# Batch 0 of a fused cross-attention and SiLU MLP kernel: loads issued ahead of a hold, one state loaded in fp32, the first activation split, and a rewritten order of two matmul streams

## The chip, the cores and the metric

The kernel runs on one core of one Trainium2 chip. The core has five engines that run side by side: TensorE (PE, with its weight loads shown as PEld), VectorE (DVE), ScalarE (ACT), GpSimd (POOL) and SyncE (SP, which here only issues transfers). They wait for one another through semaphores. The metric is the device time of one execution in microseconds (us); lower is better. A profiled execution gives a trace whose span is a little shorter than that time.

## What is computed

```python
# x: (8, 8, 512, 64)  batch, head, token, depth      state: (8, 8, 32, 64)
a  = softmax(x @ state^T / 8);   xread = a  @ state          # 512 rows of each head
a2 = softmax(state @ x^T / 8);   sread = a2 @ x              # 32 rows of each head
X  = concat([xread, sread], rows), heads side by side        # (8 * 544, 512)
h  = X @ w_in                    # w_in  (512, 2048)
out = (h * sigmoid(h)) @ w_out   # w_out (2048, 512), out (4352, 512), fp32
```

## The kernel before

**Folding.** For the 512 token rows of a batch, h = a @ (state @ w_in). The kernel forms W1[b] = state @ w_in (256 rows, heads times states, by 2048) and multiplies the normalised attention weights by it, so that only 256 rows are summed where w_in has 512. `w1_mms` and `w1_out` make W1 in column pieces of 512 (one piece needs the same columns of w_in; ScalarE and VectorE copy it out of PSUM).

**G1 and G2.** The 2048 columns are 16 slices of 128 (`ft`). `emit_G1(k)` makes slice k: two matmuls of 512 columns into a PSUM tile (two buffers take turns), and a silu on ScalarE into `g`. `upto(k)` emits all slices below k that are still to do. `G2(0, tt, ft)` multiplies 128 rows (`tt` 0 to 3) of slice ft by w_out and adds to one of four PSUM tiles. Batch 0 takes this plain form, because its weights are still arriving. From batch 1 on, G2 is a two-level Strassen-like product: `t_weights` and `inner_weights` make differences of w_out on VectorE once, and the `Unit` class runs seven products, their steps threaded between the next G1 by a list `todo` of (product, step, earliest slice).

**Order.** The schedule is by hand: each engine runs its instructions in the order of the program text. The start is lines 176 to 281. SP loads x[0] in two halves of four heads (L186). GpSimd makes the identity, sets columns of ones beside x[0] (`ones_beside_x`, L193), issues w_in columns 0 to 255 and 256 to 511, w_out slices 0 and 1, and state 1, which is cast to bf16 while it is loaded (L197). Then a one-element copy, `after_casts` (L279), reads the last piece of x[0] that VectorE casts; it holds GpSimd's queue until that is there. Behind it come w_out 2 and 3 and w_in 512 to 1023 (L280, 281), then two parts of the softmax normalisation of batch 0 (`an`, L400), then w_out 4 to 7, w_in 1024 on, x[1], and the rest of the weights (L874 to 883). There are eight semaphores for GpSimd's loads, so that each load from the ninth on waits for the landing of the one eight before it.

`g1_first` (L536) makes the first two slices, with a silu of 512 columns each. The loop at L908 then goes through slices 0 to 11 of batch 0. `LEAD0` says how far G1 runs ahead, `W0` and `W1_AT` at which slice a W1 piece of batches 0 and 1 is made (before slices 3, 6 and 11), `T3` when the fourth row tile takes its G2. The transposes, scores and exponentials of batch 1 stand at slices 8 to 10. After the loop come the remaining G2 and four G1 slices with transposes of batch 1's attention weights between them; then four `inner_weights`, of which two are made here (L956) and two in batch 1 (L1059).

Of the kernel before, what the change touches and what calls it, by code (L numbers as in the profile page):

```python
# [22 lines left out]
D = 64  # L23
# [19 lines left out]
def kernel(  # L43
# [37 lines left out]
    ident = pers.tile([128, 128], BF16)  # L81
    st_b = pers.tile([128, 8, 2 * D], BF16)
    st0_f = pers.tile([128, 2, D], FP32)
    st1_n = pers.tile([128, 2, D], BF16)
    st0_n = pers.tile([128, 2, D], BF16)

# [32 lines left out]
    def ones_beside_x(i, eng):  # L119
        eng.memset(  # L120
            x_rows[i][:, 0 : 16 * XW].rearrange("p (i w) -> p i w", w=XW)[:, :, 0:PAD], 1.0
        )
        eng.memset(x_rows[i][:, ds(16 * XW, PAD)], 1.0)
# [32 lines left out]
    def load_w_in(f, n=512):  # L156
        nc.gpsimd.dma_start(w_in_sb[:, :, ds(f, n)], win_re[:, :, ds(f, n)])

    def load_w_out(g0, n):
        nc.gpsimd.dma_start(w_out_sb[:, ds(g0, n), :], wout_re[:, ds(g0, n), :])  # L160
# [24 lines left out]
    for hg in range(2):  # L185
        nc.sync.dma_start(  # L186
            x_f[0][:, ds(4 * hg, 4), :, :],
            x[0, ds(4 * hg, 4)].rearrange("h (p c) d -> p h c d", p=128, c=4),
        )
    nc.vector.memset(stT[:, 0], 0.0)  # L190
    nc.vector.memset(stT[:, 1:8], 0.0)
    make_identity(nc, ident)
    ones_beside_x(0, nc.gpsimd)  # L193
    load_w_in(0, 256)
    load_w_in(256, 256)
    load_w_out(0, 2)
    nc.gpsimd.dma_start(  # L197
        st1_n.rearrange("p v d -> p (v d)"),
        state[1].rearrange("h (m v) d -> (h m) (v d)", v=2),
    )  # L200

    both = (nc.vector, nc.scalar)

    def load_states():
        nc.gpsimd.dma_start(
            st_b[:], state.rearrange("b h (n2 m v) d -> (b h n2) m (v d)", n2=2, m=8)
        )
# [69 lines left out]
        cast_x(0, eng, c, n, 4, 4)  # L277
    after_casts = pers.tile([128, 1], BF16)
    copy(nc.gpsimd, after_casts[:], x_nat[0][:, 2, 3, 127:128])  # L279
    load_w_out(2, 2)  # L280
    load_w_in(512)

    st_x = pers.tile([128, 8, B, 4, 2, 2], BF16)

# [199 lines left out]
    def w1_mms(b, cols, new=bank):  # L484
        pss = {}
        if b not in W1:
            W1[b] = wpool.tile([128, 2, DF], BF16, tag="W1", name="W1")
        for f, n in cols:
            for hg in range(2):
                pss[f, hg] = new([128, 512], FP32, "ps_w1")  # L490
            for s in range(4):
                for hg in range(2):
                    h = HEAD_OF_SLOT[hg][s]
                    r = 64 * (h % 2)
                    nc.tensor.matmul(  # L495
                        pss[f, hg][ds(32 * s, 32), 0:n],
                        stT[ds(r, 64), b, h // 2, s % 2, :],
                        w_in_sb[ds(r, 64), h // 2, ds(f, n)],
                        start=True,
                        stop=True,  # L500
                        tile_position=(r, 32 * s),
                        skip_group_check=True,
                    )
# [15 lines left out]
    gt = {}  # L519
# [16 lines left out]
    def g1_first():  # L536
        for k in range(2):
            g_tile(k)
        pss = [
            psA.tile([128, 512], FP32, tag="a1", name="h1"),  # L540
            psH.tile([128, 512], FP32, tag="h1", name="h1"),
        ]
        for hg, c, n in ((0, 0, 4), (1, 0, 2), (1, 2, 2)):
            for k in range(2):
                nc.tensor.matmul(
                    pss[k][:, ds(128 * c, 128 * n)],
                    W1[0][:, hg, ds(128 * k, 128)],
                    aT[0][:, hg, ds(c, n), :],
                    start=(hg == 0),
                    stop=(hg == 1),  # L550
                    skip_group_check=True,
                )
        for k in range(2):
            nc.scalar.activation(gt[k], pss[k][:], func=SILU, bias=0.0)

    def g1_half(k, hg):
        b, ft = divmod(k, NFT)
# [342 lines left out]


    turn[0] = 0
    W0 = {3: (512, 512), 6: (1024, 512), 11: (1536, 512)}
    W1_AT = {3: 0, 6: 512, 11: 1024}
    LEAD0 = [3, 3, 2, 1, 4, 3, 2, 3, 4, 3, 2, 1]
    T3 = {1: (0, 1), 2: (2,), 3: (3,), 4: (4,), 5: (5,), 6: (6,), 7: (7,), 10: (8,)}
    ready = 4
    for ft in range(12):  # L908
        upto(min(ft + LEAD0[ft], ready))
        if ft == 1:  # L910
            place_one_state(1, transpose_one_state(st1_n), nc.vector)
        if ft in W0:
            pss = w1_mms(0, [W0[ft]], new_h)
            pss1 = w1_mms(1, [(W1_AT[ft], 512)])
            w1_out(0, [W0[ft]], both, pss)
            if ft == 6:
                cast_x(1, nc.vector, 2, 2, 0, 4)
            w1_out(1, [(W1_AT[ft], 512)], both, pss1)
            ready = sum(W0[ft]) // 128
        if ft == 5:  # L920
            t_weights((1,), 0, 8)
        if ft == 6:
            for hg in range(2):
                cast_x(1, nc.gpsimd, 0, 2, 4 * hg, 4)
            load_states()
            load_x(2)
            cast_x(1, nc.vector, 2, 2, 4, 4)
            load_x(3)
        if ft == 8:
            for hg in range(2):  # L930
                pe_transpose_x(1, hg, 1, engs=(nc.vector,))
            nc.scalar.activation(warm[:], busy[:, 0:1], func=EXP, bias=0.0)
        if ft in (9, 10):
            scores(1, ft - 9, new=new_h)
            exps(1, ft - 9)
        if ft == 9:
            t_weights((2, 3, 4), 0, 4)
        if ft == 10:
            nc.scalar.activation(warm[:], busy[:, 0:1], func=SILU, bias=0.0)
            norm(1, 0)  # L940
        if ft == 11:
            norm(1, 1, ((nc.vector, 0, 4),))
# [55 lines left out]
    for b in range(1, B):  # L998
# [41 lines left out]
        for j in range(lead, NFT):  # L1040
            upto(NFT * b + j + 1)
            if j == 8:
                u.hi = gh[b, 1]
            if j == max(lead, 5):
                u.sums3(0, 4)
                if b == 1:
                    transpose_x(3)
                    for v in range(2):
                        evict_state(v, (nc.vector, nc.gpsimd)[v], 2, 2)
                if inner:  # L1050
                    u.inner_sums((3,))
# [172 lines left out]
```

## Time and profile before

| what | us |
|---|---|
| median of three runs | 201.53 (201.41 to 201.54) |
| the profiled execution | 201.34 |
| its span in the trace | 199.5 |
| TensorE busy in the span | 191.3 |
| VectorE, ScalarE, GpSimd busy | 149.1, 139.0, 73.3 |
| moved by DMA over the span | 28.72 MB |

The granted TensorE clock is full in all slices of the span. Busy time counts a matmul from its start to its modelled end, and successive matmuls overlap, so a gap between two rows of the timeline can be longer than the idle time printed in brackets. A few matmul records are missing from a trace.

### The profile page before, as it was taken

The numbers are of one execution on the slowest core, as the hardware profiler recorded it, in microseconds if no ns is written. First come the engines' busy times: TensorE is split into PE (matmuls) and PEld (weight loads), VectorE is DVE, ScalarE is ACT, GpSimd is POOL, SyncE is SP. The second block draws the span as 40 slices with busy tenths as digits, with TensorE's granted clock in tenths as the row PEclk, the third lists the DMA queues.
The fourth block names the chain that finished last, engine by engine and source line by source line (L and its number), as shares of the span: only waits on it lengthen the run. The fifth ranks groups of instructions, "written<-read, shape, count | busy, mean of one in ns | idle before, by whom it ended". The sixth has DMA issues, their size and how long they took to land.

```text
span 199.5 us, 4817 instructions
## 1 busy us (share of the span) xinstructions
PE 191.3 (96%) x1962; PEld 130.3 (65%) x1980; DVE 149.1 (75%) x284; ACT 139.0 (70%) x254; POOL 73.3 (37%) x98
## 2 busy tenths in 40 slices
PE   7799999999999999999999999999999999999992
PEld 2343354467766677667766777668766876788881
DVE  3854579897899799869995879769676997673072
ACT  2865597689779797889778967889588167825530
POOL 7596452497593008500760047102400236002200
PEclk9999999999999999999999999999999999999999
DMA  5999999999459463495229930952090005000143
GB/s 187 195 168 213 294 206 321 223 298 214 150 91 275 109 214 58 165 228 189 53 108 218 259 59 0 291 97 52 4 264 3 5 12 210 3 0 0 41 174 105
DMA packets 40839, 28.72 MB, mean 144 GB/s; under 512 B 27377, under 2 KB 37489, under 8 KB 40817
## 3 DMA queue, kind: packets, MB, share of 16 engines
q1 hardware_dynamic: 34592, 20.52, 39.3%
q0 software_dynamic: 5936, 7.64, 18.7%
q8 instruction: 15, 0.25, 0.5%
q10 hardware_dynamic: 288, 0.26, 0.4%
q14 instruction: 8, 0.06, 0.1%
HBM read 17.43 MB, written 8.91 MB: 132 GB/s over the span
## 4 chain that ended last, share of the span: by engine, by line
PE 76%; DMA 13%; DVE 6%; issue 1%; ACT 1%; POOL 0%; SPq 0%; DVEq 0%; ACTq 0%
PE o L686 35%; PE h L560 21%; DMA w_in_sb<-in_moe_w_in_dram 10%; PE h L578 4%; PE ps_w L495 3%; PE o L749 3%; DMA x_f<-in_x_dram 3%; DVE W L166 2%; PE o_ch L749 2%; PE o_s L806 2%; DVE g L611 2%; PE o L806 1%; PE ps_sr L434 1%; PE o_a L597 1%; PE o L597 1%
## 5 line engine op out<-in xcount | busy, mean ns | idle before, releaser
L588 ACT ACTIVATE g<-h 128x512 bf16<-128x512 f32 (+1 forms) x142 | 80.0, 574 | 30.2 <-PE h L560 13.0
L560 PE MATMUL h<-aT,W 128*128 128x512 bf16 x237 | 69.7, 379 | 0.2
L686 PEld LDWEIGHTS <-g 128*128 128x128 bf16 x464 | 44.8, 98 | 20.9 <-DVE kept L614 0.7
L686 PE MATMUL o<-w_out_sb,g 128*128 128x256 bf16 x336 | 49.0, 273 | 0.4
L614 POOL TENSOR_TENSOR o_sb<-o_sb,kept 128x512 f32<-128x512 f32 x7 | 10.3, 1473 | 76.3 <-ACT o_sb L164 76.3
L560 PEld LDWEIGHTS <-W 128*128 128x128 bf16 x252 | 23.1, 98 | 7.5 <-issue 0.9
L686 PE MATMUL o<-wt,s 128*128 128x256 bf16 x224 | 27.3, 273 | 0.0
L686 PEld LDWEIGHTS <-s 128*128 128x128 bf16 x224 | 21.5, 98 | 4.5 <-issue 2.1
L166 DVE CAST W<-ps_w 128x512 bf16<-128x512 f32 (+1 forms) x34 | 21.1, 665 | 3.3 <-PE ps_w L495 3.2
L164 ACT ACTIVATE W<-ps_w 128x512 bf16<-128x512 f32 (+1 forms) x32 | 16.8, 582 | 7.9 <-PE ps_w L495 7.9
L166 POOL CAST x_nat<-x_f 128x512 bf16<-128x512 f32 x24 | 16.0, 707 | 6.2 <-DMA x_f<-in_x_dram 6.2
L614 DVE TENSOR_TENSOR o_sb<-o_sb,o 128x512 f32<-128x512 f32 x14 | 9.6, 683 | 11.2 <-PE o L686 7.5
L686 PE MATMUL o<-wt,g 128*128 128x256 bf16 x128 | 16.8, 273 | 0.0
L611 DVE TENSOR_TENSOR g<-g 128x1024 bf16<-128x1024 bf16 x15 | 11.2, 744 | 6.5 <-ACT g L588 6.3
L164 ACT ACTIVATE o_sb<-o 128x512 f32<-128x512 f32 x15 | 8.9, 595 | 8.7 <-PE o L686 4.5
L614 POOL TENSOR_TENSOR o_sb<-kept,o_sb 128x512 f32<-128x512 f32 x7 | 9.2, 1311 | 15.4 <-ACT o_sb L164 15.4
L611 DVE TENSOR_TENSOR g<-g,s 128x1024 bf16<-128x1024 bf16 x14 | 14.4, 1071 | 0.0
L611 DVE TENSOR_TENSOR s<-g 128x512 bf16<-128x512 bf16 (+3 forms) x23 | 11.0, 508 | 0.0
L749 PEld LDWEIGHTS <-inner 128*128 128x128 bf16 x96 | 7.3, 98 | 5.4
L495 PE MATMUL ps_w<-w_in_sb,stT 64*32 64x512 bf16 (+1 forms) x264 | 10.2, 375 | 0.6 <-DMA w_in_sb<-in_moe_w_in_dram 0.5
L597 PEld LDWEIGHTS <-g 128*128 128x128 bf16 x64 | 5.7, 98 | 7.0 <-issue 1.2
L614 DVE TENSOR_TENSOR s<-s,g 128x1024 bf16<-128x1024 bf16 x15 | 9.7, 686 | 0.0
(123 smaller groups left out, 256.3 us busy)
## 6 DMA issues: line engine op xcount, KB each, us to landing
out_dram<-o_sb SPq DMA_DIRECT2D x14, 512.0 KB, 2.8
x_f<-in_x_dram SPq DMA_DIRECT2D x6, 512.0 KB, 5.2
w_out_sb<-in_moe_w_out_dram POOLq DMA_DIRECT2D x8, 256.0 KB, 9.5
x_f<-in_x_dram POOLq DMA_DIRECT2D x2, 1024.0 KB, 11.9
x_f<-in_x_dram SPq DMA_DIRECT2D x2, 1024.0 KB, 5.8
w_in_sb<-in_moe_w_in_dram POOLq DMA_DIRECT2D x3, 512.0 KB, 9.2
x_f<-in_x_dram POOLq DMA_DIRECT2D x2, 512.0 KB, 10.3
out_dram<-o_sb SPq DMA_DIRECT2D x4, 256.0 KB, 6.0
```

The lines of the kernel that those rows point to most:

```text
L164: nc.scalar.activation(dst, src, func=COPY, bias=0.0)
L166: eng.tensor_copy(dst, src)
L495: nc.tensor.matmul(pss[f, hg][ds(32 * s, 32), 0:n], stT[ds(r, 64), b, h // 2, s % 2, :], w_in_sb[ds(r, 64), h // 2, ds(f, n)], start=True, ...
L560: nc.tensor.matmul(h_ps[k][:], W1[b][:, hg, ds(128 * ft, 128)], aT[b][:, hg, :, :], start=(hg == 0), stop=(hg == 1), skip_group_check=True,)
L578: nc.tensor.matmul(ps[:, 0:256], w_in_sb[:, kt, ds(128 * ft, 128)], xmT[:, :, kt].rearrange("p t n b -> p t (n b)"), start=(kt == 0), stop ...
L588: nc.scalar.activation(gt[k], ps[:, 0:n], func=SILU, bias=0.0)
L597: nc.tensor.matmul(outs[tt][:], gt[b * NFT + ft][:, ds(128 * tt, 128)], w_out_sb[:, ft, :], start=(ft == 0), stop=(ft == NFT - 1), skip_gr ...
L611: eng.tensor_tensor(dst, a, c, op=SUB)
L614: eng.tensor_tensor(dst, a, c, op=ADD)
L686: nc.tensor.matmul(to[:, t, :], left[:, ds(128 * t, 128)], right[:, k, :], start=first and t == 0, stop=(k == 7), skip_group_check=True,)
L749: nc.tensor.matmul(to, left[:, k], right[:, k], start=where not in self.begun, stop=(k == 3), skip_group_check=True,)
L806: nc.tensor.matmul(to[:, 0:n], left[:, k], right[:, k, ds(c, n)], start=(first and k == 0), stop=(k == 7), skip_group_check=True,)
```

## The change

1. Of GpSimd's start, the columns of ones go to VectorE. In front of the hold stand now five weight loads (w_in 0 and 256, w_out 0 to 3, w_in 512), behind it w_out 4 to 7. State 1 is loaded in fp32 by SP after x[0]; GpSimd casts it after the normalisation.
2. The first silu of `g1_first` is two instructions of 256 columns.
3. The tables of the batch 0 loop are replaced. W1's columns 1024 are made after the first G2 of slice 6 and columns 1536 after the fourth row tile's slice 7, behind the loop; that tile's slices 6 to 11 all move behind the loop. At slice 8 each half of batch 1's transposes follows a pair of G1.
4. Batch 0's two `inner_weights` join those of batch 1. In batch 2 step 4 of product 1 moves ahead, from slice 13 to slice 9.

```diff
-    make_identity(nc, ident)
-    ones_beside_x(0, nc.gpsimd)
+    nc.sync.dma_start(
+        st1_f.rearrange("p v d -> p (v d)"),
+        state[1].rearrange("h (m v) d -> (h m) (v d)", v=2),
+    )
...
+    ones_beside_x(0, nc.vector)
+    make_identity(nc, ident)
     load_w_in(0, 256)
     load_w_in(256, 256)
     load_w_out(0, 2)
-    nc.gpsimd.dma_start(
-        st1_n.rearrange("p v d -> p (v d)"),
-        state[1].rearrange("h (m v) d -> (h m) (v d)", v=2),
-    )
+    load_w_out(2, 2)
+    load_w_in(512)
...
     copy(nc.gpsimd, after_casts[:], x_nat[0][:, 2, 3, 127:128])
-    load_w_out(2, 2)
-    load_w_in(512)
+    load_w_out(4, 2)
+    load_w_out(6, 2)
...
-        for k in range(2):
-            nc.scalar.activation(gt[k], pss[k][:], func=SILU, bias=0.0)
+        for k, c, n in ((0, 0, 256), (0, 256, 256), (1, 0, 512)):
+            nc.scalar.activation(
+                gt[k][:, ds(c, n)], pss[k][:, ds(c, n)], func=SILU, bias=0.0
+            )
...
-    load_w_out(4, 2)
-    load_w_out(6, 2)
+    copy(nc.gpsimd, st1_n[:], st1_f[:])
     load_w_in(1024)
...
-    W0 = {3: (512, 512), 6: (1024, 512), 11: (1536, 512)}
-    W1_AT = {3: 0, 6: 512, 11: 1024}
-    LEAD0 = [3, 3, 2, 1, 4, 3, 2, 3, 4, 3, 2, 1]
-    T3 = {1: (0, 1), 2: (2,), 3: (3,), 4: (4,), 5: (5,), 6: (6,), 7: (7,), 10: (8,)}
-    ready = 4
+    def w_pieces(f, f1):
+        pss = w1_mms(0, [(f, 512)], new_h)
+        pss1 = w1_mms(1, [(f1, 512)])
+        w1_out(0, [(f, 512)], both, pss)
+        if f == 1024:
+            cast_x(1, nc.vector, 2, 2, 0, 4)
+        w1_out(1, [(f1, 512)], both, pss1)
+
+    UPTO = {0: 3, 1: 4, 4: 8}
     for ft in range(12):
-        upto(min(ft + LEAD0[ft], ready))
+        upto(UPTO.get(ft, 0))
...
+        if ft == 3:
+            w_pieces(512, 0)
...
         if ft == 8:
-            for hg in range(2):
-                pe_transpose_x(1, hg, 1, engs=(nc.vector,))
+            upto(10)
+            pe_transpose_x(1, 0, 1, engs=(nc.vector,))
+            upto(12)
+            pe_transpose_x(1, 1, 1, engs=(nc.vector,))
...
         for tt in range(3):
             G2(0, tt, ft)
-        for i in T3.get(ft, ()):
-            G2(0, 3, i)
-    transpose_states()
-    for ft in (9, 10):
+            if ft == 6 and tt == 0:
+                w_pieces(1024, 512)
...
+        if 0 < ft < 6:
+            for i in ((0, 1) if ft == 1 else (ft,)):
+                G2(0, 3, i)
+    for ft in range(6, 12):
         G2(0, 3, ft)
+        if ft == 7:
+            w_pieces(1536, 1024)
+            norm(1, 1, ((nc.vector, 0, 4),))
+            transpose_states()
     upto(14)
     pe_transpose_a(1, 0, nc.vector)
-    G2(0, 3, 11)
     upto(16)
     pe_transpose_a(1, 1, nc.vector)
     t_weights((3, 2, 4), 4, 4)
-    for i in (0, 1):
-        inner_weights(i, nc.vector)
...
-            todo = [(1, k - 8, k + 4) for k in range(4)] + [(7, 1, 8)]
+            todo = [(1, k - 8, k + 4) for k in range(4)] + [(7, 1, 8), (1, -4, 9)]
...
-            todo += [(1, k - 8, (k + 23) // 2) for k in range(4, 8)]
+            todo += [(1, k - 8, (k + 23) // 2) for k in range(5, 8)]
...
-                    for i in (2, 3):
+                    for i in range(4):
                         inner_weights(i, nc.vector)
```

More of the change, by code (lines that the diff above doesn't have):

```diff
@@ L83 @@
     st0_f = pers.tile([128, 2, D], FP32)
+    st1_f = pers.tile([128, 2, D], FP32)
     st1_n = pers.tile([128, 2, D], BF16)
@@ L902 @@
     turn[0] = 0
-    W0 = {3: (512, 512), 6: (1024, 512), 11: (1536, 512)}
-    W1_AT = {3: 0, 6: 512, 11: 1024}
-    LEAD0 = [3, 3, 2, 1, 4, 3, 2, 3, 4, 3, 2, 1]
-    T3 = {1: (0, 1), 2: (2,), 3: (3,), 4: (4,), 5: (5,), 6: (6,), 7: (7,), 10: (8,)}
-    ready = 4
+    def w_pieces(f, f1):
[6 more added lines that the diff above has]
+    UPTO = {0: 3, 1: 4, 4: 8}
     for ft in range(12):
-        upto(min(ft + LEAD0[ft], ready))
+        upto(UPTO.get(ft, 0))
         if ft == 1:
             place_one_state(1, transpose_one_state(st1_n), nc.vector)
[L912 to L919, printed above, removed]
+        if ft == 3:
+            w_pieces(512, 0)
         if ft == 5:
             t_weights((1,), 0, 8)
-        if ft == 6:
-            for hg in range(2):
[L924 to L928, printed above, removed]
         if ft == 8:
-            for hg in range(2):
-                pe_transpose_x(1, hg, 1, engs=(nc.vector,))
+            upto(10)
+            pe_transpose_x(1, 0, 1, engs=(nc.vector,))
+            upto(12)
+            pe_transpose_x(1, 1, 1, engs=(nc.vector,))
             nc.scalar.activation(warm[:], busy[:, 0:1], func=EXP, bias=0.0)
@@ L940 @@
             norm(1, 0)
-        if ft == 11:
-            norm(1, 1, ((nc.vector, 0, 4),))
         for tt in range(3):
             G2(0, tt, ft)
-        for i in T3.get(ft, ()):
-            G2(0, 3, i)
-    transpose_states()
-    for ft in (9, 10):
+            if ft == 6 and tt == 0:
+                w_pieces(1024, 512)
+                for hg in range(2):
+                    cast_x(1, nc.gpsimd, 0, 2, 4 * hg, 4)
+                load_states()
+                load_x(2)
+                cast_x(1, nc.vector, 2, 2, 4, 4)
+                load_x(3)
+        if 0 < ft < 6:
+            for i in ((0, 1) if ft == 1 else (ft,)):
+                G2(0, 3, i)
+    for ft in range(6, 12):
         G2(0, 3, ft)
+        if ft == 7:
+            w_pieces(1536, 1024)
+            norm(1, 1, ((nc.vector, 0, 4),))
+            transpose_states()
     upto(14)
     pe_transpose_a(1, 0, nc.vector)
-    G2(0, 3, 11)
     upto(16)
```

## The prediction

> **What bounds the kernel now.** I read the page's busy table first, then the chain of waits, then TensorE's timeline at the places where the chain leaves TensorE.
>
> ```profile
> PE 191.3 (96%) x1962; PEld 130.3 (65%) x1980; DVE 149.1 (75%) x284; ACT 139.0 (70%) x254; POOL 73.3 (37%) x98
> ```
>
> TensorE has work for 96% of the span, so a gain can only be a gap on TensorE that closes. In the chain (start, length, what) the gaps lie in batch 0, where it runs through loads:
>
> ```profile
> 1.26 5.25 DMA x_f<-in_x_dram
> ...
> 8.13 7.99 DMA w_in_sb<-in_moe_w_in_dram
> ...
> 16.41 12.83 DMA w_in_sb<-in_moe_w_in_dram
> ```
>
> The second half of x[0] lands at 6.51 us, w_in columns 512 to 1023 at 16.12, the last columns at 29.24. TensorE's timeline shows what each costs (start, length, line, tiles; in brackets idle time and what ended it):
>
> ```profile
> 12.67 0.61 PE L597 MATMUL o<-w_out_sb,g 128*128 128x512 bf16 x2
> ...
> 15.33 0.59 PE L597 MATMUL o_a<-w_out_sb,g 128*128 128x512 bf16 x2
> 16.16 0.63 PE L495 MATMUL ps_w<-w_in_sb,stT 64*32 64x512 bf16 x16 [0.24 <-DMA w_in_sb<-in_moe_w_in_dram]
> ...
> 17.59 1.89 PE L560 MATMUL h<-aT,W 128*128 128x512 bf16 x8
> 19.32 0.59 PE L597 MATMUL o<-w_out_sb,g 128*128 128x512 bf16 x2
> ...
> 20.62 0.59 PE L597 MATMUL o_a<-w_out_sb,g 128*128 128x512 bf16 x2
> 21.49 0.62 PE L495 MATMUL ps_w<-w_in_sb,stT 64*32 64x512 bf16 x16 [0.28 <-DMA w_in_sb<-in_moe_w_in_dram]
> ...
> 28.60 0.59 PE L597 MATMUL o_a<-w_out_sb,g 128*128 128x512 bf16 x2
> 29.29 0.63 PE L495 MATMUL ps_w<-w_in_sb,stT 64*32 64x512 bf16 x16
> ...
> 64.47 1.27 PE L560 MATMUL h<-aT,W 128*128 128x512 bf16 x4
> ```
>
> Eight matmuls from 17.59 to 19.32 give 0.216 us each; a printed length of 0.38 for the last of a row is pipeline. So TensorE was ready for W1's columns 512 at 15.33 + 0.43 = 15.76 and began at 16.16: 0.40 lost. For 1024 it was ready at 21.05 and began at 21.49: 0.44. For 1536, ready 29.03, begun 29.29: 0.26. Together **1.10 us**, all three behind a w_in load. What feeds the loads (the windows' last column is GB/s):
>
> ```profile
> 6.50:9.50 3.00, 2.35 (x34) 1.42 (x35) 2.57 (x7) 2.90 (x8) 2.07 (x4) 1.00 1.36 190
> 9.50:12.50 3.00, 2.57 (x25) 1.26 (x24) 2.37 (x8) 2.14 (x4) 3.00 (x5) 1.00 1.14 159
> 12.50:15.00 2.50, 2.44 (x13) 1.14 (x13) 0.92 (x4) 1.70 (x4) 2.50 (x4) 1.00 1.14 179
> ...
> 17.50:19.50 2.00, 2.00 (x11) 0.88 (x9) 0.78 (x2) 1.52 (x4) 0.89 (x2) 1.00 1.24 207
> ```
>
> ```profile
> 1.25 0.31 POOL L120 MEMSET x_rows<- 128x256 bf16 x1
> 1.50 0.11 POOL L123 MEMSET x_rows<- 128x16 bf16 x1
> 1.55 1.70 POOL L157 DMA_DIRECT2D w_in_sb<-in_moe_w_in_dram  x2
> 3.22 0.73 POOL L160 DMA_DIRECT2D w_out_sb<-in_moe_w_out_dram  x1
> 3.91 0.60 POOL L197 DMA_DIRECT2D st_n<-in_state_dram  x1
> 7.31 0.19 POOL L166 COPY after_casts<-x_rows 128x1 bf16<-128x1 bf16 x1 [2.80 <-DVE x_rows L166]
> 7.43 0.72 POOL L160 DMA_DIRECT2D w_out_sb<-in_moe_w_out_dram  x1
> 8.13 0.78 POOL L157 DMA_DIRECT2D w_in_sb<-in_moe_w_in_dram  x1
> 9.04 1.80 POOL L400 TENSOR_TENSOR an<-exp_nat,rc 128x512 bf16<-128x512 bf16 x2
> 10.78 1.48 POOL L160 DMA_DIRECT2D w_out_sb<-in_moe_w_out_dram  x2
> 12.25 0.76 POOL L157 DMA_DIRECT2D w_in_sb<-in_moe_w_in_dram  x1
> ...
> 16.41 0.77 POOL L157 DMA_DIRECT2D w_in_sb<-in_moe_w_in_dram  x1 [0.45 <-DMA w_in_sb<-in_moe_w_in_dram]
> ```
>
> GpSimd issues four loads, waits 2.80 us at the hold, issues two, computes, and goes on at 10.78. The transfers run below their 207 GB/s for 5.5 us: (207 - 159) x 3.0 + (207 - 179) x 2.5 = 214 KB, or 1.0 us of loading. This is where the change works.
>
> **The loads (cost 0 on GpSimd, worth up to 1.10).** The two memsets go to VectorE, so the first issue starts 0.30 earlier (1.25). Issues then run 1.25 to 2.95 (w_in twice), to 4.40 (w_out twice), to 5.2 (w_in 512): about 3 us earlier than 8.13. After the hold two w_out issues (1.44) take the time that two took before (1.50), so the normalisation at 9.04 is not moved. Behind it stands the new copy of state 1: the same cast takes 0.35 on VectorE (row below); on GpSimd I take 0.25 to 0.5. Then w_in 1024 goes out at about 11.2 instead of 12.25 and everything behind it a microsecond earlier; the last w_in issue still waits for w_in 512 to land, as at 16.41, and moves with it. State 1's load leaves this queue (0.60 of issue) for SP's, behind both x halves; nothing stands behind it there before the state transposes much later, and no one needs it before its own transpose near 13.7.
>
> So each w_in landing moves by at least the 0.30, and by 0.30 + 1.0 if the dip was lack of queued loads. I take 0.9, nearer the upper end, because the two worst windows are those in which GpSimd issued nothing or had only just resumed. The three waits need 0.4, 0.6 and 0.7: TensorE reaches columns 1024 at 15.76 + 4.89 + 0.22 (one G2 matmul now ahead of them) = 20.87, against 21.45 before; and 1536 at 20.87 + 7.54 + 0.22 = 28.63, against 29.24. All three fall: **-1.10** (lower end -0.48, worked out under the first rival).
>
> **x[0] pays for the earlier start: +0.10.** The first w_in loads share the DMA engines with x[0]'s second half for 0.30 us more; the bounds are 0 and those whole 0.30. The fourth and fifth load lie behind three others in one queue and cannot yet touch x[0].
>
> The Trainium skill, page DMA: Bandwidth & Descriptors, section Queues, rings and completion order, says that every DMA engine takes turns between the queues that have work for it, packet by packet. By that rule half of the 0.30 is lost, 0.15, and the sum below would be -0.92; no view here splits queues over time, so no row confirms it.
>
> **First silu in halves: -0.10.**
>
> ```profile
> 9.02 0.65 ACT L164 ACTIVATE W<-ps_w 128x256 bf16<-128x256 f32 x2
> 12.02 1.09 ACT L554 ACTIVATE g<-h 128x512 bf16<-128x512 f32 x2 [0.83 <-PE h L545]
> ...
> 28.98 1.28 ACT L939 ACT_TABLE_LOAD   x1
> ...
> 30.39 1.06 ACT L164 ACTIVATE W<-ps_w 128x512 bf16<-128x512 f32 x2
> ```
>
> In the changed program both halves wait for the last matmul into that tile, so neither starts before 12.02. Two 256-column activations take 0.65 together, of which the first is about 0.38 by my estimate: the first G2 moves from 12.67 to about 12.45. But the second tile's silu now ends at about 13.17 instead of 13.11, and the G1 after the first three G2 needs its buffer: it goes at about 13.22 where it went at 13.33. Bounds 0 and -0.22.
>
> **New order of G1 and G2: +0.35.** W1's columns 1024 stand one G2 later, 1536 two; this moves work and adds none. What it takes away is filler between G1 pairs. G1 has two buffers; the third G1 of four can start when the first one's silu is done, 0.43 + 0.16 + 0.60 = 1.2 after that G1 began. After columns 1536 only four transposes (0.22) stand between the pairs, so TensorE is there after 1.08: 0.15 lost, with 0.05 more on the fourth and 0.05 at the same pattern around slice 8. **+0.25** (0 to 0.5). ScalarE's copy of W1 at 30.39 starts 1.10 after 29.29 because of the table load; two G2 later it starts 0.67 after, ends before the four G2 (0.86) and the W1 matmuls are through, and costs 0 (to 0.13).
>
> The transposes of x[1] also come three matmuls sooner.
>
> ```profile
> 23.07 0.86 POOL L166 CAST x_rows<-x_f 128x512 bf16<-128x512 f32 x1 [2.37 <-DMA x_f<-in_x_dram]
> ```
>
> ```profile
> 3.64 0.35 DVE L166 CAST st_n<-st_f 128x128 bf16<-128x128 f32 x1 [1.42 <-DMA st_f<-in_state_dram]
> ...
> 23.03 0.43 DVE L166 CAST x_rows<-x_f 128x512 bf16<-128x512 f32 x1 [0.38 <-DMA x_f<-in_x_dram]
> 23.37 0.68 DVE L166 CAST W<-ps_w 128x512 bf16<-128x512 f32 x1
> ...
> 35.82 0.42 DVE L611 TENSOR_TENSOR wt<-wt 128x512 bf16<-128x512 bf16 x1
> ...
> 46.59 0.69 DVE L166 COPY kept<-o 128x512 f32<-128x512 f32 x1 [1.12 <-PE o L686]
> ```
>
> Their PSUM bank is free when the copy at 23.37 ends, 24.05, which is 2.56 after W1's 1024 matmuls (21.49); GpSimd's cast ends 2.44 after. TensorE now asks 0.56 + 9 x 0.216 = 2.50 after: **+0.10** (0 to 0.3).
>
> **VectorE: 0.** The two memsets (0.42 on GpSimd) fit in its idle 1.42 before 3.64. Two inner_weights subtractions of 0.42 leave the stage before the stores and join batch 1's, in front of the copy at 46.59, which waits 1.12 for TensorE: 0.84 is covered. If that cover shrank by TensorE's gain of a microsecond, the copy would come up to 0.7 late, but the state transposes VectorE waits for there move with the loads as well.
>
> **Batch 2's moved product step: -0.22.** Four G1 matmuls from 64.47 last 1.27 - 0.16 = 1.11 where 0.86 would do: 0.25 is waiting for silu. The step put between (two 256-column matmuls, 0.22) fills it; where it came from, the G1 then follows directly and its buffer is free.
>
> **Sum.** -1.10 + 0.10 - 0.10 + 0.25 + 0.10 - 0.22 = **-0.97**. The profiled execution took 201.34 (span 199.5 and 1.84 around it), 0.19 under the median of 201.53. 201.34 becomes 200.37; against the median, **200.6**. A measurement of this kernel tells about 0.2%, 0.4 us, from no change.
>
> **Rivals.** *The loads land no earlier.* For it: the DMA share stays at 1.14 even in the 159 GB/s window, so the engines may be slow rather than short of work. The waits would be 0.40 at 512, then ready 16.16 + 4.89 + 0.22 = 21.27 against 21.45: 0.22 at 1024, and none at 1536 (21.49 + 7.76 = 29.25). Saved 0.48 instead of 1.10, no x[0] payment: -0.97 + 0.62 - 0.10 = -0.45, **201.1**; with landings 0.2 late, 201.3. Against it: at 207 GB/s the same engines do more. 20%.
>
> *x[0]'s second half is held up: slower.* The five loads keep the weights' queue full from 1.25 on, and x[0] lands not at 6.6 but d later; casts, transposes, scores, exp and GpSimd's hold all follow 6.51 directly. With the waits gone the time is 200.6 + (d - 0.1): no gain from d = 1.0, slower by over 0.4 from d = 1.4. At d = 1.5, **202.0**. Against it: x[0]'s transfers began near 1.3 and the weights' before were issued at 1.55, and 6.51 was still reached. 12%.
>
> *The gain is given back in batch 1.* The VectorE work put ahead of 46.59, or states and x[2] landing late, would keep TensorE waiting there; 0.7 back gives **201.3**. 8%.
>
> The silu halves may do nothing; that is 0.10, inside the range.
>
> **Numbers.** Forecast 60% (0.58 faster, 0.02 same). First rival 20%: 0.05, 0.13, 0.02 for faster, same, slower. Second 12%: slower 0.10, same 0.02. Third 8%: same 0.04, faster 0.02, slower 0.02. Faster 0.65, same 0.21, slower 0.14. The range: down to -1.42, with no new wait and nothing paid by x[0] (200.1), up to 201.8, which leaves most of the second rival out. The forecast's own range is 200.1 to 201.1.
>
> **What would show it.** Right: the W1 rows at 512, 1024 and 1536 start without a DMA wait, about 15.7, 20.9 and 28.7; w_in 512 lands before 15.6; 9.5 to 12.5 moves 190 GB/s or more; x[0]'s second half lands at 6.5 to 6.8; the first G2 at 12.5; small gaps among the G1 of slices 12 to 15. Wrong: x[0] landing after 7.5, the normalisation later than 9.3, a DMA wait still ahead of W1, or a new VectorE wait near 46.

## The result and the profile after

The changed kernel takes 200.51 us (200.39 to 201.03, six runs) where the kernel before, beside it, takes 201.47 (200.98 to 201.77): a ratio of 0.9959, 95% interval 0.9943 to 0.9975, or 0.8 us less (0.5 to 1.15); the two medians are 0.96 apart. The forecast was 200.6. Its profiled execution is the longest of the six, 201.03 with a span of 199.3.

The busy times of the changed kernel, and its windows over the loads (start and end, length, busy time of TensorE, its weight loads, VectorE, ScalarE and GpSimd, granted clock, DMA share, GB/s):

```profile
PE 191.9 (96%) x1962; PEld 130.3 (65%) x1980; DVE 149.6 (75%) x286; ACT 138.8 (70%) x255; POOL 72.0 (36%) x96
```

```profile
9.50:12.50 3.00, 2.51 (x25) 1.26 (x24) 2.70 (x9) 2.14 (x6) 3.00 (x5) 1.00 1.24 206
12.50:15.00 2.50, 2.50 (x13) 1.04 (x12) 0.72 (x4) 2.21 (x5) 2.50 (x4) 1.00 1.24 206
```

The dip is gone: 206 GB/s where there were 159 and 179. What GpSimd issues, and when (its timeline; start, length, line):

```profile
1.43 1.69 POOL L158 DMA_DIRECT2D w_in_sb<-in_moe_w_in_dram  x2
3.10 1.43 POOL L161 DMA_DIRECT2D w_out_sb<-in_moe_w_out_dram  x2
4.49 0.79 POOL L158 DMA_DIRECT2D w_in_sb<-in_moe_w_in_dram  x1
...
9.49 1.79 POOL L403 TENSOR_TENSOR an<-exp_nat,rc 128x512 bf16<-128x512 bf16 x2 [0.38 <-DVE rc L401]
11.24 0.28 POOL L167 CAST st_n<-st_f 128x128 bf16<-128x128 f32 x1
11.48 0.81 POOL L158 DMA_DIRECT2D w_in_sb<-in_moe_w_in_dram  x1
```

w_in 512 is issued at 4.49 instead of 8.13 and lands at 14.54 instead of 16.12; columns 1024 land at 20.15 and 1536 at 27.96, both 1.3 earlier than before. On TensorE's timeline the three W1 pieces no longer wait for a load:

```profile
15.67 0.59 PE L602 MATMUL o_a<-w_out_sb,g 128*128 128x512 bf16 x2
16.19 0.63 PE L498 MATMUL ps_w<-w_in_sb,stT 64*32 64x512 bf16 x16
...
21.08 0.38 PE L602 MATMUL o<-w_out_sb,g 128*128 128x512 bf16 x1
21.39 0.63 PE L498 MATMUL ps_w<-w_in_sb,stT 64*32 64x512 bf16 x16
...
28.52 0.81 PE L602 MATMUL o_a<-w_out_sb,g 128*128 128x512 bf16 x3
29.26 0.63 PE L498 MATMUL ps_w<-w_in_sb,stT 64*32 64x512 bf16 x16
```

Each of them starts 0.31 after the last G2 matmul before it has started, with its columns 1.2 to 1.7 us in SBUF. Yet in this execution they start hardly earlier than before (16.16, 21.49, 29.29). One reason is the new order, which puts one more G2 matmul ahead of the second piece and two ahead of the third. The other lies ahead of them all: the head, which is the work before the first G1, was slow. Here is a second profile of the same program (200.32, span 198.6) against the first one. `ps_busy` are filler matmuls that only keep TensorE busy. The first profile:

```profile
4.64 1.03 PE L173 MATMUL ps_busy<-busy 128*128 128x512 bf16 x2
5.68 1.03 PE L260 MATMUL ps_xt<-ident,x_rows 128*128 128x128 bf16 x8
...
11.50 1.04 PE L548 MATMUL h<-aT,W 128*128 128x512 bf16 x6
```

and the second:

```profile
4.52 0.61 PE L173 MATMUL ps_busy<-busy 128*128 128x512 bf16 x2
5.45 0.71 PE L260 MATMUL ps_xt<-ident,x_rows 128*128 128x128 bf16 x8 [0.32 <-DVE x_rows L167]
...
10.95 1.04 PE L548 MATMUL h<-aT,W 128*128 128x512 bf16 x6
```

In the first, x[0] landed 0.3 later (6.79 against 6.45), TensorE was still slow at 4.64 (two fillers in 1.03 against 0.61) and its first transposes took 1.03 against 0.71; the first G1 began 0.55 later. As the program is the same, that is chance between executions, not the change. So the experiments are compared by two stretches that leave the head out: from the first G1 matmul to the first state product of batch 1 (`ps_sr`), and from there to that of batch 2. The first is 41.25 before (11.05 to 52.30) and 40.56 after (11.50 to 52.06). In the second profile the three pieces start at 15.64, 20.84 and 28.78, where the prediction had 15.7, 20.9 and 28.7.

### The profile page after: what moved, and what is told of

It reads as the page before. It is cut to its first block, busy times and chain, and to the rows that moved or that the text cites. A ratio compares the mean times of both kernels' runs of the same rounds, so it can differ in the third digit from the quotient of the medians.

```text
span 199.3 us, 4817 instructions
## 1 busy us (share of the span) xinstructions
PE 191.9 (96%) x1962; PEld 130.3 (65%) x1980; DVE 149.6 (75%) x286; ACT 138.8 (70%) x255; POOL 72.0 (36%) x96
## 3 DMA queue, kind: packets, MB, share of 16 engines
HBM read 17.43 MB, written 8.91 MB: 132 GB/s over the span
## 4 chain that ended last, share of the span: by engine, by line
PE 94%; DVE 1%; ACT 1%; issue 1%; POOL 1%; POOLq 0%
PE o L691 39%; PE h L565 25%; PE ps_w L498 4%; PE h L583 4%; PE o L602 4%; PE o_a L602 3%; PE o L754 3%; PE o_ch L754 2%; PE ps_busy L173 2%; PE o_s L811 2%; PE o L811 1%; PE ps_sr L437 1%; PE ps_xt L260 1%; PE ps_at L419 1%; PE ps_sc L317 1%
```

## The experiments

Four kernels ran on one chip, then four on another, then three, then one, each group beside the kernel before. All ratios are to that. The stretches are read from the start of the first `h` row and of the `ps_sr` rows on TensorE's timeline, in one profiled execution of each. Two profiles of one program differ in the first stretch by 0.22 (before) and 0.07 (changed), in the second by 0.14 and 0.20, so a difference of that size between two kernels is no finding by itself.

| kernel | median us | before | ratio (95%) | first G1 to ps_sr 1 | to ps_sr 2 |
|---|---|---|---|---|---|
| changed, again | 200.41 | 201.04 | 0.9971 (0.9960 to 0.9982) | 40.63 | 59.67 |
| loads only | 200.46 | 201.04 | 0.9969 (0.9958 to 0.9981) | 40.47 | 59.73 |
| order, no loads | 201.13 | 201.04 | 1.0009 (0.9996 to 1.0022) | 40.83 | 59.98 |
| first silu whole | 200.54 | 201.04 | 0.9978 (0.9964 to 0.9991) | 40.67 | 59.71 |
| loads and halves | 200.43 | 201.03 | 0.9966 (0.9955 to 0.9977) | 40.36 | 60.09 |
| loads ahead only | 200.62 | 201.03 | 0.9977 (0.9965 to 0.9990) | 40.47 | 59.73 |
| state 1, ones only | 200.95 | 201.03 | 0.9999 (0.9987 to 1.0010) | 40.98 | 59.88 |
| before, again | 200.84 (one run) | 201.03 | | 41.03 | 59.72 |
| loads, halves, step | 200.28 | 201.33 | 0.9948 (0.9935 to 0.9962) | 40.36 | 59.68 |
| changed, old step | 200.39 | 201.33 | 0.9958 (0.9945 to 0.9971) | 40.56 | 59.83 |
| two loads ahead | 200.53 | 201.26 | 0.9967 (0.9953 to 0.9981) | 40.51 | 59.73 |

**The changed kernel again**, without an edit.

> The changed kernel a second time, for a second profile. In its first profile x[0]'s second half landed at 6.79 us, 0.28 later than before, and TensorE's clock came to full at 6.9 instead of 4.8; by the theory that both are chance at the start of an execution, this run is 0.9 to 1.2 us under the kernel before (ratio about 0.995), x[0] lands within 6.4 to 6.7 and the first G2 starts at about 12.5. By the rival that the earlier weight loads hold x[0] up, it lands at 6.7 or later again and the first G2 stands at 12.8 or later.

It is 0.6 us under before, on another chip: the gain is there, but smaller than at first and than the 0.9 to 1.2 expected. x[0] landed at 6.45 and the first G2 stood at 12.36, so the late x[0] of the first profile was chance.

**The loads alone.** The kernel before with the new head of GpSimd's queue, state 1 on SP and its cast; order and silu as before.

```diff
+    nc.sync.dma_start(
+        st1_f.rearrange("p v d -> p (v d)"),
...
+    ones_beside_x(0, nc.vector)
     make_identity(nc, ident)
-    ones_beside_x(0, nc.gpsimd)
...
-    nc.gpsimd.dma_start(
-        st1_n.rearrange("p v d -> p (v d)"),
...
+    load_w_out(2, 2)
+    load_w_in(512)
...
-    load_w_out(2, 2)
-    load_w_in(512)
+    load_w_out(4, 2)
+    load_w_out(6, 2)
...
-    load_w_out(4, 2)
-    load_w_out(6, 2)
+    copy(nc.gpsimd, st1_n[:], st1_f[:])
...
```

> The kernel before with the new loads alone (five ahead of the hold, ones on VectorE, state 1 in fp32 through SP), with the old order, whole silu and old places of the other steps. If the three waits on w_in (0.40, 0.44, 0.26) were lack of queued loads, they all go here already, w_in 512 lands near 14.5, and the time falls by 0.8 to 1.1 us, less what x[0] pays. If the new order is what makes the difference, the time stays within 0.3 of before.

The loads give the whole gain, 0.6 us, which is less than the 0.8 to 1.1 expected. w_in 512 lands at 14.58. TensorE's timeline of this kernel:

```profile
15.36 0.59 PE L600 MATMUL o_a<-w_out_sb,g 128*128 128x512 bf16 x2
15.89 0.63 PE L498 MATMUL ps_w<-w_in_sb,stT 64*32 64x512 bf16 x16
...
20.34 0.59 PE L600 MATMUL o_a<-w_out_sb,g 128*128 128x512 bf16 x2
20.87 0.63 PE L498 MATMUL ps_w<-w_in_sb,stT 64*32 64x512 bf16 x16
...
27.98 0.59 PE L600 MATMUL o_a<-w_out_sb,g 128*128 128x512 bf16 x2
28.50 0.63 PE L498 MATMUL ps_w<-w_in_sb,stT 64*32 64x512 bf16 x16
```

**The order without the loads.** The changed kernel with the edit just shown taken back, state 1 and the columns of ones included; in part:

```diff
...
-    load_w_out(2, 2)
-    load_w_in(512)
...
-    load_w_out(4, 2)
-    load_w_out(6, 2)
+    load_w_out(2, 2)
+    load_w_in(512)
...
-    copy(nc.gpsimd, st1_n[:], st1_f[:])
+    load_w_out(4, 2)
+    load_w_out(6, 2)
```

> The changed kernel with the old loads: order, silu halves, moved VectorE work and batch 2's step stay. By the first rival's sum (the loads land no earlier) the waits are 0.40, 0.22 and 0: 0.3 to 0.5 us under before. If order and loads only work together, it is not faster than before.

The time is that of the kernel before: 1.0009, an interval on both sides of 1, and not the 0.3 to 0.5 us of the first rival's sum. With the old loads W1's columns 1024 still begin only when they land (20.98; W1 at 21.02).

**The first silu whole again**, in the changed kernel.

```diff
-        for k, c, n in ((0, 0, 256), (0, 256, 256), (1, 0, 512)):
+        for k in range(2):
...
```

> The changed kernel with the first silu whole again. Both halves wait for the last matmul into the tile, so by my sum the halves are worth 0.1 us: this run is 0 to 0.2 us over the changed kernel. The rival: the extra instruction delays the second tile's silu, on which the next G1 waits, and the whole silu is the same or 0.05 faster; the first G2 then starts 0.2 later and the G1 behind it at the same distance from the last h matmul.

The first G2 stands 1.63 after the first G1 (10.99 to 12.62), against 1.41 with halves (10.95 to 12.36): 0.22 at that place. Of this 0.04 is left by batch 1 in this pair, and 0.11 in the pair of the old order (40.47 against 40.36). The time (200.54 against 200.41) says nothing of so little.

**Loads and halves, old order.** The kernel before with the loads' edit above and the halves of the diff above, and nothing else.

> The kernel before with the new loads and the first silu in halves, in the old order of G1, G2 and W1. If loads and halves add up and the new order is worth nothing (my theory): 0.10 to 0.12 under the loads alone, so 0.6 to 0.8 us under the kernel before, level with the changed kernel or up to 0.15 better; the first G2 at about 12.4, and W1's rows at 512, 1024 and 1536 without a load's landing ahead of them. Rival, that the halves need the new order: level with the loads alone, first G2 still near 12.7 or the gain gone by the first product of batch 1.

It is level with the changed kernel, without any of the rewritten order. Batch 0 is the shortest of all (40.36), but 0.3 comes back in the next stretch, 60.09. VectorE's timeline there:

```profile
59.66 1.22 DVE L377 TENSOR_REDUCE rs<-e 128x32 f32<-128x1024 bf16 x1 [0.40 <-DMA e<-eT]
```

It waits for a transposing DMA on SP's queue that carries batch 2's attention. In the loads-only kernel the same DMA was issued 0.5 earlier and VectorE did not wait. The early batch 0 is not the reason: the kernel with the step below comes as early (40.36), has this DMA issued at 55.94 instead of 56.26, and does not wait.

**Only the place of the issues.** The kernel before with w_out 2 and 3 and w_in 512 ahead of the hold, w_out 4 to 7 behind it; state 1 and the columns of ones stay on GpSimd.

```diff
         state[1].rearrange("h (m v) d -> (h m) (v d)", v=2),
     )
+    load_w_out(2, 2)
+    load_w_in(512)
...
-    load_w_out(2, 2)
-    load_w_in(512)
+    load_w_out(4, 2)
+    load_w_out(6, 2)
...
-    load_w_out(4, 2)
-    load_w_out(6, 2)
```

> The kernel before with nothing changed but the place of two issues: w_out 2 and 3 and w_in 512 stand ahead of the hold, w_out 4 to 7 right behind it; state 1 is still cast while it is loaded on GpSimd's queue, and the columns of ones stay on GpSimd. If the dip of the transfers was a lack of queued loads (my theory): 200 GB/s or more from 9.5 to 12.5, w_in 512 landing at 14.7 to 15.1, 0.3 to 0.6 later than with all of the new loads, no wait for w_in ahead of W1, and 0.5 to 0.7 us under the kernel before. Rival, that state 1's casting load on the same queue was what slowed the transfers: the window stays under 185 GB/s, w_in 512 lands after 15.4, and the time is within 0.3 us of the kernel before.

**Only state 1 and the columns of ones** moved; the issues stay behind the hold.

```diff
+    nc.sync.dma_start(
+        st1_f.rearrange("p v d -> p (v d)"),
...
+    ones_beside_x(0, nc.vector)
     make_identity(nc, ident)
-    ones_beside_x(0, nc.gpsimd)
...
-    nc.gpsimd.dma_start(
-        st1_n.rearrange("p v d -> p (v d)"),
...
+    copy(nc.gpsimd, st1_n[:], st1_f[:])
```

> The other half of the new loads: state 1 in fp32 on the other queue with its cast behind the normalisation, and the columns of ones on VectorE, while w_out 2 and on and w_in 512 stay behind the hold. If the dip was a lack of queued loads (my theory): it stays, 150 to 180 GB/s from 9.5 to 12.5, w_in 512 lands at 15.5 to 16.2, and the time is 0 to 0.3 us under the kernel before. Rival, state 1's load or the 0.30 us of GpSimd's start: w_in 512 at 15.0 or earlier, and 0.5 us or more under the kernel before.

**The kernel before again**, for its profile.

> The kernel before once more, for its profile. If its landings differ between executions while the cause stays: w_in 512 at 15.5 to 16.2, under 180 GB/s from 9.5 to 12.5, and W1's columns 1024 and 1536 still behind a w_in load, by 0.1 to 0.5 us each. If the first profile was an odd one: no wait for w_in at all, and a span near 198.6.

The three belong together. Their rows for 9.5 to 12.5 us, in this order (place of the issues, state 1 and ones, before again):

```profile
9.50:12.50 3.00, 2.50 (x25) 1.17 (x24) 2.64 (x8) 2.14 (x5) 3.00 (x4) 1.00 1.28 204
```

```profile
9.50:12.50 3.00, 2.58 (x25) 1.26 (x24) 2.27 (x7) 2.16 (x5) 3.00 (x6) 1.00 1.12 161
```

```profile
9.50:12.50 3.00, 2.57 (x25) 1.26 (x24) 2.27 (x7) 2.16 (x5) 3.00 (x5) 1.00 1.07 163
```

The place of two issues takes the dip away and, by the ratio, 0.46 us of the time, a little under the 0.5 to 0.7 expected. w_in 512 landed at 15.29, also a little later than expected, but none of the three W1 pieces waits: each starts 0.52 after the last pair of G2. The other half of part 1 leaves the dip and the time as they were. For state 1 and ones one number missed: w_in 512 landed at 15.13, since the first piece was early (8.02), but the next one came at 21.08 as before, and TensorE waited for it.

The second profile of the kernel before corrects the first:

```profile
15.20 0.59 PE L597 MATMUL o_a<-w_out_sb,g 128*128 128x512 bf16 x2
15.75 0.63 PE L495 MATMUL ps_w<-w_in_sb,stT 64*32 64x512 bf16 x16
...
20.20 0.59 PE L597 MATMUL o_a<-w_out_sb,g 128*128 128x512 bf16 x2
21.11 0.63 PE L495 MATMUL ps_w<-w_in_sb,stT 64*32 64x512 bf16 x16 [0.31 <-DMA w_in_sb<-in_moe_w_in_dram]
...
28.22 0.59 PE L597 MATMUL o_a<-w_out_sb,g 128*128 128x512 bf16 x2
28.93 0.63 PE L495 MATMUL ps_w<-w_in_sb,stT 64*32 64x512 bf16 x16
```

Here w_in 512 landed at 15.71 instead of 16.12, and the first of the three waits is nearly nothing.

**Loads, halves and batch 2's step**, old order in batch 0.

```diff
-            todo = [(1, k - 8, k + 4) for k in range(4)] + [(7, 1, 8)]
+            todo = [(1, k - 8, k + 4) for k in range(4)] + [(7, 1, 8), (1, -4, 9)]
...
-            todo += [(1, k - 8, (k + 23) // 2) for k in range(4, 8)]
+            todo += [(1, k - 8, (k + 23) // 2) for k in range(5, 8)]
```

> The kernel before with the new loads, the silu halves and batch 2's moved step, in the old order of batch 0. If the moved step closes 0.24 at slice 13 and gives back about 0.20 behind it (my theory after the first runs): 0 to 0.1 under loads and halves, 0.6 to 0.9 under the kernel before, level with the changed kernel; batch 2's stage from the first state products of batch 1 to those of batch 2 between 59.6 and 60.1 us long. Rival, that the step is worth its 0.22 where nothing else follows it: 200.2 and 0.8 to 0.9 under the kernel before, the stage 59.5 or less.

**The changed kernel with the step back** at slice 13.

```diff
-            todo = [(1, k - 8, k + 4) for k in range(4)] + [(7, 1, 8), (1, -4, 9)]
+            todo = [(1, k - 8, k + 4) for k in range(4)] + [(7, 1, 8)]
...
-            todo += [(1, k - 8, (k + 23) // 2) for k in range(5, 8)]
+            todo += [(1, k - 8, (k + 23) // 2) for k in range(4, 8)]
```

> The changed kernel with step 4 of product 1 back at slice 13 of batch 2; all else as changed. By the prediction's term it loses 0.22, with a gap of 0.24 again in four G1 matmuls near 63.8 and no gap near 68.8. By what the first runs showed it loses 0 to 0.1: the 0.24 gap comes back, and the 0.14 near 68.8 and the 0.06 near 64.5 go.

In the first the stretch of batch 2 is 0.41 shorter than without the step (59.68 against 60.09, which has VectorE's wait of 0.40 in it), in the second pair 0.16 (59.67 against 59.83). But other kernels without the step reach 59.72 and 59.73 as well: loads only, ahead only, two ahead, before again. Over all profiles here it is 59.82 without (eight) and 59.78 with it (five). What the step moves is seen in TensorE's rows without it (the changed kernel with the old step), and in those of TensorE, its weight loads and VectorE with it (the changed kernel's second profile):

```profile
63.64 1.16 PE L565 MATMUL h<-aT,W 128*128 128x512 bf16 x4
...
68.95 1.25 PE L691 MATMUL o<-w_out_sb,g 128*128 128x256 bf16 x10
```

```profile
68.30 0.73 DVE L619 TENSOR_TENSOR kept<-kept,o 128x256 f32<-128x256 f32 x2
...
68.73 1.51 PE L691 MATMUL o<-w_out_sb,g 128*128 128x256 bf16 x11
...
69.08 0.99 PEld L691 LDWEIGHTS <-g 128*128 128x128 bf16 x10 [0.25 <-DVE kept L619]
```

Four G1 matmuls without a wait last 4 x 0.216 + 0.16 = 1.02, so the gap there was 0.14 (0.25 in the loads-only kernel). Eleven product matmuls without one last 11 x 0.108 + 0.16 = 1.35, and with the step they last 1.51: 0.16 of waiting has moved further on. The other four profiles with the step have 0.16 to 0.18 at this place. Ten in the kernel without it last 1.25, which is no wait. The releaser is VectorE: its two additions of `kept` end at 69.03, and the next product needs the PSUM tile that they empty. Without the move they end no earlier (68.31 and 0.73), but the step itself stands in front of that product and covers them.

The kernel with loads, halves and step has the lowest median, 200.28 (200.12 to 200.41); its 1.05 us under the kernel before is more than either expectation, with a kernel before that ran longer there (201.33) than on the other chips. Beside it on the same chip the changed kernel with the old step took 200.39 (200.32 to 200.72). They differ by less than the time can tell; on TensorE it is ahead of the changed kernel's second profile by 0.27 in batch 0.

**x[0] without weights beside it.** The changed kernel with its five loads behind the hold; 205.71 us in one run, since all weights come late.

```diff
-    load_w_in(0, 256)
-    load_w_in(256, 256)
-    load_w_out(0, 2)
-    load_w_out(2, 2)
-    load_w_in(512)
...
     copy(nc.gpsimd, after_casts[:], x_nat[0][:, 2, 3, 127:128])
+    load_w_in(0, 256)
+    load_w_in(256, 256)
+    load_w_out(0, 2)
+    load_w_out(2, 2)
+    load_w_in(512)
```

> The changed kernel with the five weight loads behind the hold: x[0] loads with no weights beside it. All of batch 0's weights come some 6 us later, so the time is 3 to 6 us longer; what counts is x[0]. If x[0]'s second half shares the engines packet by packet with the weights, it lands at 5.9 or earlier without them; if it is bounded by its own queue, at 6.2 to 6.5 as before.

x[0]'s second half landed at 6.35, within the 6.2 to 6.5 expected if its own queue bounds it, as its place in the chain shows:

```profile
1.26 5.09 DMA x_f<-in_x_dram
```

With the five weight loads it was 6.45. So the weights cost x[0] about 0.1 at most; the same loads landed it anywhere from 6.39 to 6.49 in the later profiles.

**Two loads ahead, nothing behind the hold.** The kernel before with w_out 2 and 3 and w_in 512 ahead of the hold, and w_out 4 to 7 where they were. Then the same five loads are under way at 9.5 us as in the kernel before (the last of w_in 256, w_out 0 and 1, state 1, w_out 2 and 3, w_in 512), only issued 2.85 earlier.

```diff
         state[1].rearrange("h (m v) d -> (h m) (v d)", v=2),
     )
+    load_w_out(2, 2)
+    load_w_in(512)
...
     copy(nc.gpsimd, after_casts[:], x_nat[0][:, 2, 3, 127:128])
-    load_w_out(2, 2)
-    load_w_in(512)
```

> The kernel before with w_out 2 and 3 and w_in 512 ahead of the hold and nothing right behind it: w_out 4 to 7 stay behind the normalisation. From 9.5 to 10.7 there are then as few loads under way as in the kernel before, or fewer, but all of them were issued by 6 us, ahead of the normalisation on GpSimd. If the dip is a lack of queued loads by number (the prediction's reason): it stays, under 185 GB/s from 9.5 to 12.5, w_in 512 lands after 15.4, and the time is within 0.3 us of the kernel before. Rival, that what counts is that a load is issued well ahead, and not some 1 us ahead of GpSimd's own work: 198 GB/s or more from 9.5 to 12.5, w_in 512 at 14.8 to 15.4, and 0.3 to 0.6 us under the kernel before.

GpSimd's issues of the two, and the windows:

```profile
4.46 0.75 POOL L160 DMA_DIRECT2D w_out_sb<-in_moe_w_out_dram  x1
5.16 0.82 POOL L157 DMA_DIRECT2D w_in_sb<-in_moe_w_in_dram  x1
```

```profile
9.50:12.50 3.00, 2.56 (x26) 1.26 (x24) 2.47 (x8) 2.14 (x5) 3.00 (x5) 1.00 1.26 204
12.50:15.00 2.50, 2.44 (x12) 1.05 (x12) 0.82 (x4) 1.80 (x4) 2.50 (x4) 1.00 1.24 205
15.00:17.50 2.50, 2.50 (x26) 0.94 (x25) 1.17 (x3) 1.03 (x2) 2.44 (x4) 1.00 1.15 178
```

The dip is gone with no more loads in the queue than before, and the time falls as with all of the new loads, by 0.7 us, a little more than expected. The rival holds: it is not their number but that they were issued well ahead. A dip of the same kind stands later, 178 GB/s from 15 to 17.5, when the loads issued from 10.89 on have their turn.

## Why the prediction was right, and where it was off

The forecast of faster held, and the reason that carried it: the three waits ahead of W1 go because the loads land earlier. The loads alone show it, and so does the place of two issues alone. The terms of the sum, one by one:

**The loads, -1.10: right mechanism, size too large.** The stretch of batch 0 shortens by 0.56 from the second profile of before to the loads-only kernel (41.03 to 40.47), and by 0.78 from the first (41.25). Two things made 1.10. First, TensorE was called ready 0.43 after the start of the last pair of G2. The loads-only kernel, where no load is late, begins W1 0.53, 0.53 and 0.52 after that pair: the turn from G2 to W1 costs 0.1 by itself, and three times 0.09 to 0.1 was counted as waiting. Without it the first profile's waits are 0.30, 0.34 and 0.16, together 0.80. Second, they were read from one execution. In the other they are 0.02, 0.38 and 0.18 by the same rule (0.55, 0.91 and 0.71 less 0.53), together 0.58. These two sums are, within 0.02, the two gains that were measured. Two smaller figures were off as well: GpSimd's first load was issued at 1.43, 0.12 earlier and not 0.30, and the third wait needed 0.61 by the prediction's own times (29.24 less 28.63), not 0.7.

**The reason for the dip: wrong as it was put.** The prediction took it for a lack of queued loads. With the same five loads issued and not yet landed the transfers ran at 204 GB/s when w_in 512 had been issued at 5.16, and at 163 when it had been issued at 8.01. Issuing at that time does not slow them either: the kernel with only the place of the issues changed issues two loads from 7.32 to 8.74 and runs at 204. Still the DMA engines were in part without a packet to move. The rows for 9.5 to 10.5 us, before again and then two loads ahead:

```profile
9.50:10.50 1.00, 0.59 (x7) 0.34 (x7) 0.76 (x3) 0.98 (x2) 1.00 (x2) 1.00 0.82 118
```

```profile
9.50:10.50 1.00, 0.56 (x6) 0.23 (x4) 0.90 (x3) 0.98 (x3) 1.00 (x2) 1.00 1.30 200
```

The DMA share (packets overlap, so that it can pass 1) is 0.82 against 1.30. In the first profile of before it falls to 0.99 at 131 GB/s, from 11.5 to 12.5. So in part fewer packets were under way, though loads had been issued; the first rival's argument, a share of 1.14 in the slow window, was a mean over three microseconds. What holds back a load that is issued shortly ahead of its turn is not shown; GpSimd's normalisation and VectorE's reductions run then in every kernel. The Trainium skill, page DMA: Bandwidth & Descriptors, section SWDGE vs HWDGE vs iDMA, says that GpSimd writes the descriptors of its loads into SBUF and that VectorE in its two-port mode locks it out there. That would fit a load whose descriptors are written while VectorE works, but the issue itself lasts 0.78 in the one kernel and 0.82 in the other, so no row here shows it.

**x[0], +0.10: right at its lower bound.** 6.39 to 6.49 with the new loads (6.79 in the first profile alone), 6.39 to 6.51 with the old ones, 6.35 with none. By the rule of turns between queues that the prediction takes from the Trainium skill (page DMA: Bandwidth & Descriptors, section Queues, rings and completion order) it was to be 0.15. Here the two queues hardly move data at the same time (last section).

**Silu halves, -0.10: it fits**, with 0.22 at the place itself and 0.11 and 0.04 left by batch 1. Two profiles of the changed kernel differ by 0.07, so the size is not shown more closely than that.

**The new order, +0.35 with the transposes of x[1]: right in kind, a little high.** In batch 0 it costs 0.27 (changed against loads, halves and step) and 0.20 (silu whole against loads only). The time is too coarse for it: 200.54 against 200.46 in the second pair. The predicted gap after columns 1536 is there, in the changed kernel's second profile:

```profile
31.07 0.39 PE L419 MATMUL ps_at<-ident,an 128*128 128x128 bf16 x4
31.49 1.08 PE L565 MATMUL h<-aT,W 128*128 128x512 bf16 x4
```

Four transposes of 0.055 end at 31.29; the next pair of G1 begins at 31.49, 0.20 late, where 0.15 was forecast (the prediction's own 1.2 less 1.08 is 0.12). With the old loads the order gains nothing that is clear of the spread either: batch 0 takes 40.83, the silu halves included, against 40.98 to 41.25 in the three profiles with old loads and old order; the next stretch is longer, 59.98 against 59.72 to 59.88.

**Batch 2's step, -0.22: the step that failed.** The gap at slice 13 closes, but 0.16 reappears behind it, and over all profiles 0.04 is left, less than they tell. The prediction said that where the step came from the next work follows directly and its buffer is free; but the step had been the cover of VectorE's two additions, which free the tile of the next product.

**VectorE, 0: right.** Two more subtractions stand ahead of the copy that was in doubt. In the changed kernel's first profile it still waits for TensorE:

```profile
46.35 0.69 DVE L167 COPY kept<-o 128x512 f32<-128x512 f32 x1 [0.23 <-PE o L691]
```

Its wait shrank from 1.12 to 0.23, by 0.89 where 0.84 was forecast. But these, too, are two single executions: the wait was 0.50 in the second profile of before and 0.10 in the second of the changed kernel, and with the old step the copy starts (45.79) as soon as VectorE is free. TensorE's matmuls follow one another without a gap there in both, so the cost is 0, with nothing left in hand.

With what was measured the sum is -0.56 to -0.78 for the loads, -0.1 for the halves, +0.2 to 0.27 for the order, about -0.04 for the step: -0.4 to -0.7 in the place of -0.97; measured were 0.6 and 0.8 us. Counted from the median before, 201.53, that would have been 200.8 to 201.1, so that 200.6 met 200.51 so closely is in part luck. The two largest gains, the loads and the step, were put 0.3 to 0.5 and 0.2 too high; the order and x[0] were put about 0.1 each too dear, which gives back less than half of it. The rest is the first comparison itself, in which the kernel before ran longer (201.47) than beside the later kernels (201.03 to 201.33).

The rivals: loads that land no earlier are refuted by the landings (14.54 and 14.98 in the changed kernel's two profiles against 15.71 and 16.12), a held-up x[0] by 6.45. The gain given back later did not come near VectorE's copy at 46, but in one execution at 59.66, 0.3 us of it. One mark of the prediction misled: the normalisation later than 9.3 was to mean that it was wrong, and it began at 9.49 in the first profile, through the slow head, and at 8.94 in the second.

## What to carry to other kernels

Read a wait from two executions before it becomes a term, and take the turn between two kinds of matmul from a place where nothing is late. Moving one issue ahead of other work on its queue can be worth more than a rewritten order that works around its late landing; do the cheap one first, alone, and see what is left for the other. Work that is moved into a gap leaves a place behind: ask what it covered there.

## What the runs showed of the hardware

**The weights come when x[0] is nearly through.** In the changed kernel the first weight load is issued at 1.43 us, but its queue moves nothing up to 5 us. The prediction said that no view splits the queues over time; the view of the DMA queues does so when it is given a window. From 2 to 5 us of the second profile (packets, MB, share of 16 engines) it has only SP's and ScalarE's queues, and SP's has moved 0.92 of x[0]'s 1.05 MB:

```profile
q1 hardware_dynamic: 912, 0.92, 87.1%
q10 hardware_dynamic: 115, 0.05, 6.3%
```

And the transfers from 3 to 5 us are as fast with the five weight loads issued as without any; first the changed kernel, then the one that holds them back:

```profile
3.00:4.00 1.00, 1.00 (x4) 0.17 (x2) 0.35 (x1) 0.00 (x0) 1.00 (x3) 1.00 1.09 385
4.00:5.00 1.00, 1.00 (x7) 0.26 (x6) 0.00 (x0) 0.00 (x0) 1.00 (x2) 1.00 1.09 379
```

```profile
3.00:4.00 1.00, 1.00 (x4) 0.17 (x2) 0.23 (x1) 0.00 (x0) 0.00 (x0) 1.00 1.10 386
4.00:5.00 1.00, 1.00 (x7) 0.26 (x6) 0.07 (x1) 0.01 (x1) 0.00 (x0) 1.00 1.08 371
```

When nothing else loads, the first weight packet comes 1.65 after the issue began (7.26 to 8.91). Beside x[0] it takes 3.3 to 4.0, and what holds it then is not shown.

**The head varies.** The profile's row of the granted clock prints full in all slices, but TensorE does not start at full pace. In both profiles of the changed kernel the first seven fillers of 512 columns stand 0.42 apart, twice the 0.216 of later matmuls. In the second profile the pace is full at 4.52 (two fillers in 0.61), in the first the fillers are slow up to 6.5, and the same eight transposes take 0.71 and 1.03. The mean granted clock over the span is 1.000 in the second and 0.997 in the first. Landings of w_in 512 with the same issues differ by up to 0.7 us between executions (14.34 to 15.07 with the new loads). The kernel before ranged from 200.42 to 201.95 us in these runs, a wider range than the gain of the change.
